# The same steps of a fused attention and MLP kernel in another written-out order

## The chip, the cores and the metric

One core of a Trainium2 chip. The metric is the device time of one execution in microseconds; a version's time is the median of several runs. TensorE does the matmuls, VectorE (DVE) and ScalarE (ACT) the elementwise work, GpSimd (POOL) issues the loads that change the type on the way, and SyncE (SP) issues the stores and the transposing loads.

## The reference

```python
def _attn_ref(q, k, v, tau):                       # 4 x 6080 x 256 each
    qn = q / (np.linalg.norm(q, axis=1, keepdims=True) + 1e-06)
    kn = k / (np.linalg.norm(k, axis=1, keepdims=True) + 1e-06)
    s = kn.transpose(0, 2, 1) @ qn / tau           # 256 x 256 per batch
    s = s - s.max(-1, keepdims=True)
    a = np.exp(s)
    a /= a.sum(-1, keepdims=True) + 1e-09
    return (v @ a).astype(np.float32)

def _moe_ref(x, w_in, w_out):                      # 24320 tokens, 256 -> 2048 -> 256
    h = x @ w_in
    c = np.float32(np.sqrt(2.0 / np.pi))
    g = 0.5 * h * (1.0 + np.tanh(c * (h + 0.044715 * h * h * h)))
    return (g @ w_out).astype(np.float32)
```

The output of the first, as 24,320 rows of 256, is the input of the second.

## The kernel before

**Tiling.** Per batch, q and k are read in pieces of 512 rows, cast to bf16 while they are loaded (`load_one`, L243), and summed up on TensorE into a 256 x 256 product (`gram_row`, L290) and, over squares on ScalarE and VectorE (L253) and folds on VectorE (L272), into column norms. A short chain of small steps turns these into the 256 x 256 attention matrix, which is multiplied into the first MLP matrix (`aw_part`, `aw_copy`, L497 to L515). So the rest is an MLP over v: 25 blocks of at most 1,024 tokens, each in two halves `t` of 512 (480 and fewer at a batch's end).

**One block.** v is cast to bf16 into a DRAM buffer by GpSimd (`cast_v`, L306) and from there loaded with a transposition by SP (`load_vt`, L319). The first matrix product is done either piece by piece (`j` steps, L553, with their GELU `J` on ScalarE, L564) or in sets that spend seven matmuls in place of eight (`small`, L613, with the steps of `set_step`, L636, on ScalarE and VectorE; they need sums of weights, L587, and differences of v, `vs0` to `vs2`, L602). The second product again spends seven products in place of eight (`product`, L727, with the differences of `sums_g`, L708). Its results are turned on VectorE in blocks of 32 x 32 (`turn`, L764, L768) into an output buffer `ot`, and SP stores a half with four issues of 128 KB (`store`, L771, L782). There are three `ot` buffers (L70), so the turn that begins a fourth half waits until the store of an earlier one has landed.

**What sets the order.** Everything after the first batch's attention runs in the order of one text, `ORDER` (L962), of 4,017 steps, worked off by the loop at L951. Each engine executes its own instructions in that order, and waits at each for what it needs; so do the queues of GpSimd and SP. A step is written `block:step` or `bN:step` for work on batch N: `14:j30` is the matmul of block 14, piece 3, half 0; `15:s3cq` is the ScalarE copy in set 3 of block 15 that opens a bank; `13:c11` is the turn of one quarter of block 13's output into half 0, `c12` and `c22` go to half 1; `12:O1` is the store of block 12, half 1; `lv` is a cast of v, `lt` a transposing load, `lq` and `lk` casts of q and k. These loads are not issued at once when their buffer is free: each also waits for the matmul that stands before it in the order (`GATE`, set at L296, L537, L560, L628, L739 and used in `after`, L92):

```python
    def after(inst, gate):
        if gate is not None:
            tc.add_manual_dep(inst.ins, gate.ins.name, mybir.DependencyInfo(
                mybir.DependencyClass.Sync, mybir.DependencyReason.DATA), reason="pace")
```

So the place of a load in the text sets the time at which it goes out.

Of the kernel before, what the change touches and what calls it, by code (L numbers as in the profile page):

```python
# [967 lines left out]
0:J50 :pA12 0:J51 :pF0 0:j71 0:j41 0:j60 0:j61 0:s6ap 0:J61 1:j00 0:J60 0:s7m1 b0:w13 0:s6m7 :pF1
0:s6ax 0:J71 1:j30 0:M1A 1:J00 1:J30 0:s7m5 1:j50 0:s6m3 0:J41 0:jb0 0:s7y5 b1:lk1 0:T3a 0:M1B
0:s7cq 0:s6G1 8:lv0 0:s7m6 0:s6m4 0:s7m2 b1:r0.0 0:Jb0 b0:w01 b1:lq2 1:J50 b1:r0.1 0:T1a 0:s7ap  # L970
1:j21 0:s7m3 0:s7G0 1:j10 0:T2a :pS1 b1:lk3 0:s6Gx b1:r0.2 0:s6Gr 3:lv0 1:j51 0:s7m7 0:s7ax 1:j41
0:s7G1 1:j31 :pS4 1:J21 1:J10 b1:r0.3 1:j40 1:J41 0:x1 0:s7Gx b1:lk2 0:s7m4 :pS2 1:vs0 1:j11 b1:dk0
b1:r1.0 b1:r1.1 b1:lq3 1:J11 1:J40 0:s7Gr 0:M2A 1:s3m1 0:T3b 1:vs1 b1:r1.2 1:s3cq 0:M6A 0:T1b 2:lv0
1:s3m2 b1:zq1 b1:lk4 b1:r1.3 1:J51 1:j01 b0:w03 0:M2B 1:J01 1:J31 1:s4m1 0:T2b 1:s3m6 4:lv0 1:s3m5
:pNA 0:M5A 0:M5B 1:s3G0 b1:lq5 0:c11 1:s4m5 1:s3y5 b1:zq0 b1:r2.0 b1:r2.1 0:M6B 1:s3ap b1:r2.2
b1:lq4 1:s4cq 1:vs2 1:s4m2 0:y5 b1:r2.3 1:s3m3 1:s3m7 0:T4b b1:r3.0 b1:zk1 1:s4y5 1:s3G1 1:s4m6
1:s4G0 0:ap b1:r3.1 1:s3ax b1:lk5 0:M3A 1:s4ap b1:f0.1 1:s3m4 1:s3Gx 1:s5m1 0:T4a 1:s4m7 0:M3B
1:s5cq 1:s3Gr b1:zq2 1:s5m2 1:s4ax 0:M7A 1:s5m5 1:s4m3 1:s5G0 1:s4Gx 0:c12 b1:r3.2 1:s5m6 1:s5y5
b1:f1.1 b1:dk4 1:s4m4 1:j20 1:s6m1 0:M7B 1:s4G1 1:s4Gr 1:J20 2:lt1 1:s5ap 1:s6cq 1:s5m3 1:s5m7
1:s7m1 b1:r3.3 b1:f1.2 1:s6m5 b1:r4.0 2:lt0 1:s6m2 0:ax 1:s5G1 1:s6m6 b1:r4.1 1:s5ax 1:s6y5 1:s5m4  # L980
1:s6G0 1:s5Gx b1:dk2 0:M4A 1:s6ap 1:s6m7 1:s7m5 b1:f2.1 1:s7cq b1:r4.2 1:s6ax 1:s5Gr b1:zq3 1:T3a
1:s6m3 0:M4B 1:s7y5 0:c21 b1:r4.3 1:s7m6 1:s6m4 1:s6Gx 1:M1A 1:s7m2 1:s6G1 1:s7ap 2:j11 1:s7m7
1:s7m3 b1:lq8 1:M1B 1:T1a 1:s7ax 2:j21 1:s6Gr b1:lq6 1:s7G0 b1:zq4 1:T2a 1:s7m4 1:s7G1 b1:lk6 2:vs0
1:x1 2:j00 b1:lk7 1:s7Gr 0:c22 b1:r5.0 2:j10 1:s7Gx 2:s2m1 2:J21 3:lv1 2:vs1 1:T3b b1:lq7 2:J00
1:M2A 2:J10 2:J11 1:M2B 2:j01 1:c11 2:s2cq 2:j30 2:j20 2:s2m5 2:s2m2 2:J01 2:s2m6 2:J30 2:J20 2:s3m1
1:T1b 2:s2G0 1:M6A 1:M5A 0:O1 1:T2b 2:s2y5 2:s3cq 2:s2ap 2:s3m5 b1:zk3 2:s3y5 2:s3m6 2:s2m7 2:s2m3
2:s2G1 2:s3m2 b1:f1.3 2:vs2 1:M5B 2:s2ax b1:f3.1 2:s3G0 2:s4m1 2:s2m4 1:y5 2:s4cq 1:M6B 2:s3ap
2:s2Gr 2:s3m7 2:s4m2 b1:zk5 b1:f3.2 1:ap b1:r5.1 2:s4m6 3:lt1 b1:r5.2 b1:r5.3 2:s4m5 1:T4b b1:f3.3
1:M7A 2:s4G0 2:s2Gx 2:s4y5 1:M7B 2:s3ax b1:zq5 2:s3Gx 2:s5m5 b1:r6.0 2:s4ap 2:s3m3 2:s3G1 2:s3m4
b1:f3.4 2:s3Gr b1:f5.1 2:s4m3 2:s4G1 1:M3A 3:lt0 2:s5m1 2:s4m7 2:s5cq 1:M3B 2:s5m2 1:T4a b1:r6.1  # L990
2:s5m6 2:s5y5 b1:zq6 1:ax 2:s5G0 1:M4A 2:s4ax 3:j11 0:O0 b1:f4.1 2:s5ap 2:s4Gx 3:j31 1:c12 3:J11
# [6 lines left out]
3:s3m1 3:J21 3:j00 3:vs1 b1:zq7 3:J20 3:s2cq 3:J00 b1:r8.0 b1:lq10 3:s2y5 2:M5A 3:s2m6 2:T2b b1:r8.1
3:s2m2 3:s3cq 2:M5B 3:s2ap b1:zq8 3:s2m7 b1:f5.4 3:s3m2 3:s2G0 3:s3G0 3:vs2 3:s2m3 2:y5 b1:r8.2
3:s2G1 b1:dk8 2:M6B 3:s3m5 3:s3y5 3:j10 3:s3m6 3:s2ax 3:s2m4 1:O1 2:ap b1:f7.1 3:s3ap 3:s2Gx 2:T4a  # L1000
2:M3A 4:lt0 3:J10 3:s4m1 3:s2Gr 2:T4b 2:M3B b1:zq9 3:s3m7 3:s3ax 3:s4m5 3:s4cq 3:s4y5 b1:zk9 2:c12
2:M7A 3:s4m2 3:s3m3 b1:r8.3 3:s4m6 2:M7B 3:s4ap 3:s4G0 3:s3G1 3:s5m5 4:lt1 3:s3m4 2:ax 3:s4m3 3:s3Gx
# [6 lines left out]
3:s7Gx b1:r11.3 3:s7G1 4:j20 b1:f9.2 2:O0 3:M1A 4:s3m1 4:vs0 6:lv1 4:J00 4:J20 4:J21 3:T3b 3:M1B
b1:gc 4:s2m5 4:vs1 4:s2cq 3:s7Gr 3:x1 4:j10 4:s2y5 b2:lk2 b1:f9.3 b1:zq10 3:T1b 3:T2a 4:s2m6 4:s2m2  # L1010
3:M5A 4:s2ap 3:M5B 3:M2A 4:s2m3 b1:zq11 3:T2b 4:s2m7 3:M2B 4:J10 4:s3m5 1:O0 4:s2G1 4:s2G0 4:vs2
4:s2ax 3:M6A 4:s3cq 4:s3m6 4:s3y5 3:y5 4:s2m4 4:s2Gr 4:s3m2 4:s2Gx 5:lt1 3:M6B 4:s4m1 b1:zk11 3:c11
3:T4b 4:j11 4:s3ap 4:s3G0 4:s3m7 3:ap 4:s4m5 4:s3m3 4:J11 b1:f9.4 4:s4cq 3:M3A 3:M7A 4:s3ax 4:s4y5
4:s3G1 4:s5m1 4:s4m2 b2:lk0 b1:f11.1 6:lv0 4:s4m6 4:s4G0 b2:lq0 4:s3m4 3:T4a 3:M3B 4:s4ap 4:s5m5
# [18 lines left out]
5:s7Gr 5:s7Gx 5:M1B 6:J50 5:T3b 6:j51 6:j21 6:s3G0 7:lt1 5:M5A 5:x1 5:T1b 6:J51 4:O0 3:O0 6:J21
6:s3m5 6:s3y5 6:s3m6 6:s4cq 5:T2a 7:lt0 5:M2A 6:s4m5 5:M2B 5:T2b 6:s3ap b2:zq0 5:c11 5:M5B b2:zq1
6:vs2 5:M6A 6:s3m7 6:s3ax 6:s4y5 6:s4m6 6:s3m3 6:s4ap b2:zk1 5:M6B 6:s5m5 6:s3m4 5:y5 5:ap 6:s4m2
6:s3G1 6:s4m7 6:s3Gx 6:s4m3 5:T4a 6:s4G1 6:s4ax 6:s4G0 7:j01 5:M3A 6:s3Gr 6:s5m1 6:s5cq 5:M3B 6:s5y5
5:M7A 5:T4b b2:f1.1 6:s5m6 6:s5m2 6:s4Gx 6:s4m4 6:s6m1 7:J01 6:s5G0 6:j30 5:M7B 5:c12 b2:lq3 6:s4Gr
6:s5ap 6:s6cq 6:s5m3 6:j10 b2:dk0 6:J30 6:s6m6 6:s7m1 6:s5m7 5:ax 6:s5G1 6:s6m5 6:j31 b2:zq2 6:s5ax
# [255 lines left out]
```

## Time and profile before

| | before |
|---|---|
| median of 3 runs | 690.88 us (690.78 to 691.38) |
| profiled execution | 690.03 us, span 688.3 us |
| mean granted clock of TensorE | 0.995 |
| busy TensorE / VectorE / ScalarE / GpSimd | 663.0 / 625.6 / 635.1 / 88.2 us |
| matmul records | 3410 |
| stores of 128 KB on SP, to landing | 160, median 3.0 us |
| transposing loads on SP, to landing | 47, median 3.1 us |
| casts of 256 KB (v, k, q) on GpSimd, to landing | 37, 33, 33, median 5.1, 5.9, 5.4 us |

Busy time is the time that an engine's instructions cover; in `x4` lines of a timeline several instructions are merged. The first 37 us belong to the first batch's attention and are outside `ORDER`. GpSimd's and SP's issues are not counted as busy. The time of a transfer runs from its issue to the moment its last part has landed.

### The profile page before, as it was taken

Reading aid. Unit: us, or ns where it says so; the run is one execution under the profiler, and the core shown is the slowest. Engines: PE = TensorE matmul, PEld = TensorE weight load, DVE = VectorE, ACT = ScalarE, POOL = GpSimd, SP = SyncE. Lnnn points to the kernel's source line nnn. Section 1 sums busy time; section 2 is a strip of 40 time slices with the busy share of each in tenths; the row PEclk is TensorE's granted clock in tenths of the full one; section 3 lists DMA queues with packets and bytes.
Section 4 is the critical chain, followed back from the end, with each engine's and each line's share of the span. In section 5 each row is a group of like instructions: output and inputs, shape, how many; then the busy total and the mean of one; then the engine's idle time right before and its main releaser. Section 6 shows DMA issues by size and latency. Waiting matters only on the chain.

```text
span 688.3 us, 10199 instructions
## 1 busy us (share of the span) xinstructions
PE 663.0 (96%) x3410; PEld 334.4 (49%) x3471; DVE 625.6 (91%) x922; ACT 635.1 (92%) x1224; POOL 88.2 (13%) x163
## 2 busy tenths in 40 slices
PE   3999999999999999999999997999999999999996
...
PEclk9999999999999999999999998999999999999999
...
GB/s 241 208 264 158 106 137 159 118 129 108 78 138 104 108 163 135 170 60 147 94 65 80 173 111 118 142 90 63 75 107 62 62 57 130 54 54 84 74 49 103
DMA packets 165093, 78.80 MB, mean 114 GB/s; under 512 B 148992, under 2 KB 153472, under 8 KB 164320
## 3 DMA queue, kind: packets, MB, share of 16 engines
...
## 4 chain that ended last, share of the span: by engine, by line
PE 86%; DMA 6%; ACT 5%; DVE 1%; issue 1%; SPq 0%; POOL 0%; DVEq 0%; POOLq 0%
PE u L739 22%; PE rb L628 16%; PE j L560 13%; PE p L739 12%; PE qb L628 8%; PE c L739 5%; PE G L296 4%; PE qa L628 4%; DMA qk<-in_k_dram 2%; DMA out_dram<-ot 2%; PE awp L501 2%; DMA qk<-in_q_dram 1%; ACT g L572 1%; ACT g L662 1%; ACT qa L643 1%
## 5 line engine op out<-in xcount | busy, mean ns | idle before, releaser
L739 PEld LDWEIGHTS <-wcomb 128*128 128x128 bf16 x1400 | 136.9, 98 | 146.9 <-issue 2.7
L739 PE MATMUL u<-t,wcomb 128*128 128x512 bf16 (+3 forms) x583 | 143.3, 368 | 0.8
L560 PE MATMUL j<-vT,aw 128*128 128x512 bf16 (+2 forms) x447 | 124.0, 375 | 0.8 <-DVE aw L392 0.5
L572 ACT ACTIVATE g<-j 128x512 bf16<-128x512 f32 (+1 forms) x204 | 122.0, 661 | 2.5 <-PE j L560 2.5
L648 DVE TENSOR_TENSOR qb<-rb,yw 128x512 f32<-128x512 f32 (+2 forms) x137 | 92.6, 679 | 10.4 <-PE rb L628 5.8
L651 DVE TENSOR_TENSOR xw<-rb,yw 128x512 f32<-128x512 f32 (+2 forms) x137 | 91.4, 669 | 7.5 <-PE rb L628 5.5
L628 PE MATMUL rb<-tv,sw 128*128 128x512 bf16 (+2 forms) x269 | 97.6, 375 | 0.6 <-DVE qb L648 0.2
L662 ACT ACTIVATE g<-xw 128x512 bf16<-128x512 f32 (+2 forms) x137 | 92.8, 680 | 5.6 <-DVE xw L651 5.6
L739 PE MATMUL p<-g,wcomb 128*128 128x512 bf16 (+3 forms) x394 | 96.6, 370 | 0.6
L646 ACT ACTIVATE yw<-qb 128x512 f32<-128x512 f32 (+2 forms) x137 | 87.6, 645 | 2.4 <-PE qb L628 2.2
L643 ACT ACTIVATE qa<-rb 128x512 f32<-128x512 f32 (+2 forms) x137 | 87.8, 643 | 2.2 <-PE rb L628 1.6
L653 ACT ACTIVATE g<-qa 128x512 bf16<-128x512 f32 (+2 forms) x137 | 87.6, 648 | 1.6 <-PE qa L628 1.3
L656 ACT ACTIVATE g<-qb 128x512 bf16<-128x512 f32 (+2 forms) x137 | 87.6, 644 | 1.5 <-PE qb L628 1.2
L659 ACT ACTIVATE g<-rb 128x512 bf16<-128x512 f32 (+2 forms) x137 | 87.2, 647 | 0.8 <-PE rb L628 0.6
L628 PEld LDWEIGHTS <-sw 128*128 128x128 bf16 x548 | 53.8, 98 | 56.4 <-issue 1.7
L560 PEld LDWEIGHTS <-aw 128*128 128x128 bf16 x456 | 44.3, 98 | 45.5 <-issue 1.1
L628 PEld LDWEIGHTS <-aw 128*128 128x128 bf16 x411 | 40.3, 98 | 42.7 <-issue 0.6
L720 DVE TENSOR_TENSOR t<-g,g 128x2048 bf16<-128x2048 bf16 (+3 forms) x50 | 58.0, 1160 | 1.0 <-ACT g L662 0.9
L722 DVE TENSOR_TENSOR t<-t,g 128x2048 bf16<-128x2048 bf16 (+3 forms) x50 | 57.4, 1157 | 1.2 <-PE u L739 1.1
L712 DVE TENSOR_TENSOR g<-g 128x2048 bf16<-128x2048 bf16 (+3 forms) x50 | 58.0, 1159 | 0.3
L718 DVE TENSOR_TENSOR t<-g,g 128x2048 bf16<-128x2048 bf16 (+3 forms) x50 | 57.9, 1161 | 0.2
L628 PE MATMUL rb<-tv,aw 128*128 128x512 bf16 (+2 forms) x137 | 51.1, 376 | 4.3 <-DVE xw L651 4.1
...
## 6 DMA issues: line engine op xcount, KB each, us to landing
out_dram<-ot SPq DMA_DIRECT2D x160, 128.0 KB, 3.0
...
wst<-in_moe_w_out_dram POOLq DMA_DIRECT2D x2, 1024.0 KB, 11.4
...
```

The costliest lines, as they stand in the source:

```text
L560: GATE[0] = nc.tensor.matmul(hp[:, :n].rearrange("p (t x) -> p t x", t=2) if t == 2 else hp[:, :n], lhsT=AW[b][:, cc, fc * 128 : fc * 128 ...
L572: nc.scalar.activation(g[:, t, fc % 8, :hc], hp[:, :hc], AF.Gelu_apprx_tanh)
L628: GATE[0] = nc.tensor.matmul(acc[:, :hc], lhsT=lhs, rhs=rhs, start=i in (1, 5), stop=True, skip_group_check=True)
L643: nc.scalar.activation(Q0[m, p][:, :hc], RB[m, p][:, :hc], AF.Copy)
L646: nc.scalar.activation(YW[m, p][:, :hc], Q1[m, p][:, :hc], AF.Copy)
L648: nc.vector.tensor_add(Q1[m, p][:, :hc], RB[m, p][:, :hc], YW[m, p][:, :hc])
L651: nc.vector.tensor_add(XW[m, p][:, :hc], RB[m, p][:, :hc], YW.pop((m, p))[:, :hc])
L653: nc.scalar.activation(g[:, 0, e, :hc], Q0.pop((m, p))[:, :hc], AF.Gelu_apprx_tanh)
L656: nc.scalar.activation(g[:, 1, e, :hc], Q1.pop((m, p))[:, :hc], AF.Gelu_apprx_tanh)
L659: nc.scalar.activation(g[:, 0, e + 1, :hc], RB.pop((m, p))[:, :hc], AF.Gelu_apprx_tanh)
L662: nc.scalar.activation(g[:, 1, e + 1, :hc], XW.pop((m, p))[:, :hc], AF.Gelu_apprx_tanh)
L739: GATE[0] = nc.tensor.matmul(ACCS[m, acc][:, :hc], lhsT=wcomb[:, w, fc, :], rhs=x[:, fc, :], start=first and k_ == 0, stop=k_ == 3, skip_g ...
```

## The change

Only the text of `ORDER` differs. It holds the same 4,017 steps, each as often as before, at other places from its first line on; the functions, the buffers and the sizes are the same. Each engine's instructions are the same in number and kind and stand in another order. Two stretches of it, around the stores of blocks 12 and 13, half 1:

```diff
...
-13:s4ax 13:s4G0 b3:r4.0 b3:lq8 12:ax 13:s5G1 13:s4G1 13:s4Gx b3:r4.1 13:s4m4 b3:dk4 12:c22 13:s6m1
-13:s5ax 13:s6cq b3:r4.2 12:M4A b3:lq6 12:M4B 13:s6y5 b3:lk8 13:s6m6 13:s4Gr 13:s5Gx 13:s6m2 13:s7m5
-b3:r4.3 13:s7m1 12:O1 b3:r5.0 13:s6G0 b3:lk7 17:lv1 13:s5m4 b3:f5.1 12:c21 13:s6ap 14:j30 13:s7cq
-13:T3a 13:s6m7 b3:r5.1 b3:lq7 13:s7m2 13:s7m6 13:s7y5 13:s6ax 13:s7ap 13:s5Gr 13:s6m3 13:s7G0 14:J30
-14:j31 13:s6m4 14:j20 13:T1a 13:s6G1 13:s7m7 b3:r5.2 14:s2m1 18:lv0 13:s7m3 13:M1A 13:s6Gx 13:s6Gr
-14:J31 13:s7ax 14:s2cq b3:f3.4 13:s7m4 13:s7G1 b3:r5.3 13:M1B b3:f4.1 14:J20 14:j21 13:s7Gr b3:lk9
-b3:lq9 13:x1 14:vs0 13:s7Gx 14:s2m2 14:j01 14:vs1 14:s2m5 14:s2m6 13:M2A 13:M2B 13:T2a b3:f5.2
...
+b3:zq4 12:ax 13:s4Gx 13:s6m5 b3:f5.1 12:c22 13:s6m2 12:O1 b3:lk6 13:s5ax 13:s4m4 b3:r4.3 13:s6m6
+13:s6y5 13:s4Gr b3:lq8 12:M4A 13:s6ap b3:lk8 b3:f3.4 13:s7m1 13:s6G0 12:M4B 13:s7cq 13:s5m4 17:lv1
+12:c21 b3:f4.1 b3:r5.0 13:s7m5 b3:lq7 13:s6m7 13:s6m3 b3:r5.1 13:s7m6 14:j31 13:s5Gx 13:s7m2 13:s5Gr
+b3:r5.2 13:s6G1 13:s7y5 14:j30 13:s6ax 13:s7G0 13:s6Gx 13:s6m4 b3:lk7 13:M1A 13:s7ap 14:J31 13:s7m7
+13:s7m3 14:j20 14:s2m1 13:T3a 13:s6Gr 18:lv0 b3:r5.3 14:J30 13:s7ax 13:s7m4 13:s7G1 14:J20 13:s7Gr
+13:T1a 13:M1B 14:j21 14:s2cq 14:vs0 b3:r6.0 14:s2m5 13:x1 14:j01 14:s2m2 14:vs1 13:T2a 14:s2m6
...
+14:s6m1 14:J10 b3:r7.2 14:s4Gx 13:T4a 14:s5m7 14:s6cq 13:c12 14:s5m3 14:s5ax 14:s6m5 14:s5G1 13:O1
+17:lv0 b3:dk8 b3:lk11 13:M4A 14:s7m1 14:s6m6 14:s6y5 14:s7cq b3:lq9 14:s5m4 14:s6m2 14:s6ap 13:M4B
+14:s5Gr 14:s6G0 b3:f7.1 14:s7m6 14:s5Gx 14:s7m5 14:s6m7 14:s6m3 13:c21 b3:lk9 14:s7y5 14:s6ax
+14:s6G1 15:j21 15:j00 15:J21 b3:r7.3 15:j30 14:s7ap 14:s6m4 14:s7m3 14:T3a 14:j00 b3:f7.2 15:J00
+14:s7m7 15:j01 18:lv1 b3:lq11 14:s6Gx 14:s7ax 14:s6Gr 14:J00 15:j20 b3:r8.0 14:s7G1 b3:r8.1 14:s7m4
+15:s2m1 15:J01 14:M1A 14:s7m2 15:J30 14:s7Gx 15:J20 b3:lq10 14:T1a 15:vs0 15:s2cq b3:r8.2 14:s7Gr
+15:vs1 15:s2m5 14:M1B 14:s7G0 b3:f7.3 b3:lk10 15:j31 14:x1 15:s2m6 15:s2m2 15:j11 15:s2y5 15:s2G0
+15:J31 b3:r8.3 b3:zk9 14:M2A 15:J11 14:T2a 15:s3m5 14:T3b 14:M2B 15:s3y5 b3:r9.0 15:s3m1 15:s2ap
...
```

More of the change, by code (lines that the diff above doesn't have):

```diff
@@ L968 @@
[L968 to L991, printed above, removed]
@@ L998 @@
[L998 to L1002, printed above, removed]
@@ L1009 @@
[L1009 to L1014, printed above, removed]
@@ new lines @@
+b1:f1.3 0:M4A 1:T3a 1:s5Gr 1:s6ax 1:s7ap 1:s6m4 1:s6Gx 1:s7m2 1:s7m7 b1:zq3 1:T1a 1:s7m3 b1:lk6
+0:M4B 1:s7ax b1:f3.1 1:s6Gr 1:s7G0 b1:r4.3 1:s7G1 b1:lq6 2:j21 0:c21 2:j30 b1:lq7 b1:r5.0 1:x1 3:lv1
+1:s7Gx 1:s7m4 2:J30 2:j20 2:j01 3:lt1 1:s7Gr 1:M2A b1:f3.2 2:j10 2:J21 2:J20 2:J01 2:s2m1 1:M2B
+2:vs0 1:T3b 2:s2cq 2:J10 1:T1b 2:vs1 2:s2m5 2:j00 2:s2m6 2:s2y5 1:c11 2:vs2 2:s2m2 b1:dk4 2:s2ap
+2:j11 2:s2G0 2:J11 1:M5A 2:s3m1 1:M5B 1:T2a 1:T2b 2:s2m7 2:s2ax 2:s3m5 2:s2m3 b1:zq4 0:O0 1:M6A
+b1:r5.1 1:M6B 2:J00 2:s2m4 0:c22 1:y5 2:s3cq 2:s2G1 b1:r5.2 b1:zq5 2:s3m6 2:s4m1 2:s3m2 1:ap 1:M7A
@@ new lines @@
+2:s7m1 3:J21 b1:r6.3 3:J10 2:s7cq 2:s6m3 2:T3a 2:s6m7 2:s7m5 b1:r7.0 2:s6G1 2:s6G0 b1:f5.2 b1:r7.1
+2:s6ax b1:r7.2 2:s7m2 3:j11 2:s7m6 2:s6m4 2:s7y5 2:M1A 2:s5Gr 3:s2m1 3:J11 b1:f6.1 3:j01 2:s6Gx
+2:s7ap 2:s6Gr 5:lv0 2:s7m7 b1:f5.3 2:s7m3 2:M1B 2:s7G0 3:j00 2:T1a 2:s7G1 b1:r7.3 2:s7ax 2:s7m4
+3:J01 3:j20 2:x1 2:T2a 2:s7Gx 3:vs0 b1:zq7 b1:lq10 2:T3b 2:s7Gr 2:M2A 3:J00 3:J20 3:s2cq 2:M6A
+b1:lq11 b1:f5.4 b1:lk9 b1:zk7 3:vs1 3:j30 2:M2B 3:s2m5 3:J30 3:s2m2 2:M5A 3:s2y5 2:T1b 2:c11 b1:lk11
+2:M5B 2:T2b 3:s2G0 2:y5 3:s3m1 3:s2m6 b1:f7.1 3:s3cq 3:s2ap 3:vs2 2:M6B b1:zq9 3:s3m5 3:s3y5 2:ap
@@ new lines @@
+4:s2m2 4:s2y5 3:M5B 3:T2b b1:zq10 4:s3m1 4:J21 3:M6B 4:s3m5 4:s2G0 4:s2ap 4:s2m7 b2:lq2 3:y5 4:s3cq
+3:T4b 4:s3y5 4:vs2 3:M2B 4:s3m6 4:s2m3 4:s2ax 3:ap 3:c11 4:s2m4 b1:zk11 4:s3ap 4:s2G1 4:s2Gr 4:s3m2
+4:s3G0 4:s2Gx b2:lk2 b1:f9.4 b1:f10.1 3:M7A 4:s4m5 4:j11 4:s4m1 4:s3m3 4:s3m7 b1:f11.1 4:J11 4:s4cq
+3:M3A 4:s3ax 4:s4m6 6:lv0 4:s3G1 4:s4y5 4:s4m2 b1:f11.2 8:lv1 4:s5m1 4:s4ap 4:s3m4 b1:f11.3 4:s4G0
+4:s5cq 4:s3Gr 3:M3B 3:T4a b1:f11.4 4:s4m3 4:s5m5 4:s3Gx 6:lv1 4:s5m2 5:j11 3:M7B 4:s5y5 5:J11 4:s4m7
@@ L1033 @@
[L1033 to L1038, printed above, removed]
@@ new lines @@
+6:s7Gr 7:s2m2 7:vs0 6:j00 7:j21 b2:r1.3 9:lv0 7:vs1 7:s2m5 7:s2G0 b2:r2.0 b2:r2.1 6:J00 6:s7Gx
+7:s3m1 7:s2y5 7:J21 6:T3a 6:T1a 7:J00 b2:r2.2 6:M1A b2:r2.3 7:s2m6 7:s3cq 6:M1B 7:s3m2 b2:r3.0
+b2:lq6 7:J10 6:x1 7:j31 7:s2ap 7:s2m3 7:s3G0 b2:lq5 7:J31 7:s2m7 7:s3m6 7:s2G1 7:s3m5 7:vs2 6:M2A
+b2:lk4 7:s5m1 6:T3b 7:s2ax 6:T2a 7:s3y5 7:s3ap 6:M2B 7:s2m4 6:M5A 6:T1b 7:s2Gx b2:lk6 b2:zk3 7:s2Gr
+b2:zq3 7:s3m7 6:c11 7:s3ax 7:s3m3 7:j30 6:M5B 7:s3m4 6:T2b 7:s5cq 7:J30 6:y5 6:M6A 6:T4a b2:f3.1
+7:s5m2 7:s3Gr 7:s4m1 7:s3G1 6:M6B b2:r3.1 7:s4cq 7:s5m6 7:s4m5 7:s4m6 6:ap 7:s4m2 7:s5G0 6:T4b
@@ new lines @@
+8:j30 7:s6Gr 7:s7m4 b2:r5.2 8:J20 8:j10 7:s7G0 7:T1a 7:M1A 7:s7G1 10:lv1 8:J30 b2:lq7 8:vs0 7:s7Gr
+8:s2m1 8:J10 7:s7Gx 8:j21 8:s2cq 7:M1B b2:f5.1 8:s2m5 7:T2a 8:j01 8:J21 7:x1 8:s2m2 8:vs1 b2:f4.1
+7:T3b 8:J01 7:T1b 8:s2m6 8:s2y5 8:s2G0 b2:r5.3 b2:r6.0 8:s2ap 8:vs2 8:s3m1 7:M2A 8:s3m5 8:s3cq
+b2:r6.1 b2:r6.2 7:T2b 7:M2B 8:s3m2 8:s2m3 8:s3y5 8:s2m7 8:s2ax b2:zq8 7:M6A 8:s3G0 8:s3m6 8:s2m4
+8:s2G1 7:c11 8:s3ap b2:dk6 8:s4m1 8:s4m5 9:lt1 7:M5A 8:s3m7 b2:r6.3 8:s2Gx 8:s2Gr 7:M5B 7:T4a 8:s4y5
+8:s4cq 8:s4m6 b2:zq6 8:s4m2 8:s3m3 7:M6B 8:s3ax 8:s3m4 7:y5 8:s4ap 8:s4G0 8:s3G1 10:lt0 8:s3Gx
@@ new lines @@
+8:s7ax 9:J11 7:c21 8:s7G0 8:M1A 9:j01 7:O0 9:s2m1 b2:lk11 8:s7m3 7:c22 11:lv1 b2:zq10 8:s7m4 8:s7Gx
+9:j21 b2:r8.1 9:s2cq 8:M1B b2:r8.2 b2:f7.3 8:s7Gr 9:vs0 b2:f7.4 9:J21 8:s7G1 b2:r8.3 9:J01 9:j10
+11:lv0 9:vs1 9:J10 b3:lq2 9:vs2 9:j00 9:s2m6 b2:lq11 12:lv1 b2:r9.0 8:T3b 9:s2m5 b2:r9.1 9:s2y5
+9:s2m2 8:T2a b2:r9.2 b2:r9.3 9:J00 9:s2ap 8:T1b 8:x1 b2:zk9 8:M5A 9:s3m1 8:M2A 9:s2m3 9:s2G0 9:s2m7
+9:s2G1 b2:dk10 9:s2ax b2:zq9 8:M2B 8:M5B 8:c11 9:s2m4 9:s3m5 8:T2b b2:f9.1 9:s3cq 9:j30 9:s3m2
+b2:f9.2 8:y5 9:s2Gr b3:lk1 9:s3y5 8:M6A 9:s3G0 9:s3m6 9:J30 9:s3ap 9:s4m1 9:s4cq 8:M6B 9:s2Gx 9:s4m5
@@ new lines @@
+9:s6m3 10:J00 9:s7m6 b2:ss 9:s6ax 10:s2m1 9:s5m4 9:s7G0 9:s7ap 9:s6G1 9:s6Gx 9:s6m4 9:s7m7 10:s2cq
+9:s7m3 9:T3a 9:s6Gr 9:M1A 10:s3m1 b2:sv 9:s7ax 9:s7G1 b2:pow 10:j01 10:s2m2 9:T1a 9:s5Gr 9:s7m4
+10:s3cq 10:J01 10:j30 9:M1B 10:j10 10:vs0 10:J30 9:M5A 9:s7Gx 9:s7Gr 10:vs1 b2:kf 10:vs2 10:s3m6
+10:J10 9:T3b 10:s2m6 9:T2a 9:T1b 9:x1 10:s3m2 13:lt1 10:s2m5 8:O1 9:M2A 9:M2B 10:s2G0 10:s3m5
+10:s2y5 10:s3G0 10:j31 10:s2ap b2:kr 9:c11 10:s3y5 9:M5B 10:s2m7 10:J31 10:s3ap 10:j11 10:s2ax
+10:s2m3 9:y5 10:s3m7 10:s3m3 11:lt1 10:s4m1 10:s2G1 9:M6A 10:s3G1 10:J11 9:T2b b2:krp 10:s4m5 b2:S0
@@ new lines @@
+10:s7m6 11:J01 10:s7y5 10:s6m4 b2:rc2 10:s7m2 10:s7G0 10:M1A 10:s7ap 10:s5Gr 10:s6Gx b2:eT 10:s6m3
+11:j10 10:s7m3 10:s7m7 11:J10 10:M1B b2:aw5 12:lt1 9:c21 10:s7ax 10:T3a 10:s7m4 b2:rsum 11:vs0
+10:s7G1 10:s6Gr 10:s6G1 10:x1 10:s7Gr b2:aw7 11:j30 b2:aw3 11:J30 10:M2A 10:s7Gx b2:rs b2:aw1 10:T1a
+9:c22 b2:ac5 b2:ac3 b2:ac1 10:T3b 11:s2m1 b2:aw2 b2:aw6 b2:ac2 13:lt0 11:vs1 b2:aw0 10:M5A 11:s2cq
+b2:ac6 10:M2B b2:ac0 10:T1b 11:s2m2 11:s2G0 9:O1 b2:aw4 10:M5B b2:ac4 11:s2m5 10:T2a 12:lt0 11:s3m1
+b2:ac7 11:j21 11:s2m6 11:s3m5 10:c11 11:s2y5 10:M6A 11:vs2 10:T2b 10:y5 11:s3cq 11:s2ap 11:s3y5
@@ new lines @@
+b3:r9.1 b3:f8.1 14:T1b 14:c11 14:M6A 15:s2m7 b3:zq9 15:s2m3 15:j10 15:s3cq b3:r9.2 b3:f7.4 b3:r9.3
+16:lt1 15:s3m6 15:s2ax 15:s3m2 15:s2G1 14:M5A 15:vs2 b3:zq11 15:s3ap 15:s3G0 12:O0 14:T2b b3:f9.1
+15:s2m4 14:M5B 15:s4m1 14:M6B 15:J10 14:T4b 15:s4m5 b3:r10.0 15:s2Gr 15:s2Gx 15:s3m3 14:y5 15:s3m7
+14:ap 15:s4cq b3:r10.1 15:s4m2 15:s3ax 15:s4y5 15:s3G1 15:s4m6 14:M3A 15:s4ap 15:s4G0 15:s3m4
+15:s5m1 b3:zq10 15:s4m7 b3:dk10 15:s3Gr 14:M3B 15:s5m5 14:T4a 15:s3Gx 15:s5cq 15:s4m3 14:M7A 15:s4ax
+15:s5m6 13:O0 15:s4m4 15:s5m2 14:c12 15:s5y5 b3:f9.2 15:s4G1 15:s5ap 15:s6m5 b3:f10.1 15:s6m1 14:M7B
@@ new lines @@
+15:s7Gx 16:J01 15:x1 16:s2y5 16:vs1 16:s2G0 15:T1a 16:s2m6 16:J20 16:j31 17:lt0 15:T3b b3:sv 16:s2ap
+16:vs2 16:J31 15:M2A 16:j11 16:s3m1 16:J11 15:T1b 16:s3m5 16:j30 16:s2m7 16:s2m3 15:M2B 16:s3cq
+16:s2G1 b3:pow 16:s2ax 16:s3y5 16:s3m6 15:M5A 16:J30 16:j00 b3:kf 16:s2m4 16:s3ap 14:O0 15:T2a
+16:s2Gx b3:kr 16:J00 16:s3m2 16:s2Gr 16:s3m3 16:s3m7 15:c11 16:s3ax 16:s3G1 15:M5B b3:krp 17:lt1
+16:s4m1 15:y5 16:s5m1 16:s3G0 15:T2b 16:s3m4 16:s3Gr 16:s5m5 b3:S0 b3:S1 16:s4cq 15:T4a b3:th1
+15:M6A 16:s5cq 15:M6B 16:s4m5 16:s4m2 15:ap 16:s4m6 16:s5y5 16:s5m6 b3:th0 16:s5ap 16:s4y5 16:s5m2
```

455 lines of the change are left out of this document (215 added, 240 removed).

## The prediction

> **What bounds the kernel now.** I read the slices of the page first, then the waits, then the timeline around the one slice that stands out. The row of TensorE and the row of its granted clock:
>
> ```profile
> PE   3999999999999999999999997999999999999996
> PEclk9999999999999999999999998999999999999999
> ```
>
> After the start every slice is full but one, near 420 us, where the clock is low too. The list of waits has only two causes that hold VectorE or TensorE for over a microsecond in the main part:
>
> ```profile
> DVE ot L768 <- DMA out_dram<-ot: 6.8, 2, 5.6
> ...
> PE rb L628 <- DVE xw L651: 4.1, 1, 4.1
> ```
>
> VectorE twice waited for a store to land, because a turn (L768) writes the output buffer `ot` that the store still reads; in one case TensorE then waited for VectorE. The timelines of TensorE and of VectorE there (start, us, engine, line):
>
> ```profile
> 418.72 1.03 PE L739 MATMUL p<-g,wcomb 128*128 128x512 bf16 x4
> 423.80 0.59 PE L628 MATMUL rb<-tv,aw 128*128 128x512 bf16 x1 [4.06 <-DVE xw L651]
> ...
> 427.46 1.65 PE L739 MATMUL p<-g,wcomb 128*128 128x512 bf16 x4
> 428.95 0.38 PE L628 MATMUL rb<-tv,sw 128*128 128x512 bf16 x1
> ```
>
> ```profile
> 416.48 0.41 DVE L611 TENSOR_TENSOR tv<-vT,tv 128x512 bf16<-128x512 bf16 x1
> 422.46 0.72 DVE L768 STREAM_TRANSPOSE ot<-c 128x512 f32<-128x512 f32 x1 [5.56 <-DMA out_dram<-ot]
> ```
>
> A 512-column matmul starts every 0.216 us at full clock, so TensorE should have gone on at 419.59 and did at 423.80: **4.21 us**. Windows of 1 us (busy, count, granted clock, DMA share, GB/s) show what follows:
>
> ```profile
> 421.00:422.00 1.00, 0.00 (x0) 0.94 0.26 46
> 422.00:423.00 1.00, 0.00 (x0) 0.50 0.01 2
> ...
> 428.00:429.00 1.00, 1.00 (x5) 0.64 0.90 170
> ```
>
> From about 421.9 to 428.7 the clock is halved. Between 423.80 and 428.95 stand nine 512-column and six 256-column matmuls, 2.59 us at full clock, that took 5.15: **2.56 us** more. The other store wait is smaller, near 259 (VectorE):
>
> ```profile
> 258.76 0.72 DVE L768 STREAM_TRANSPOSE ot<-c 128x512 f32<-128x512 f32 x1 [1.22 <-DMA out_dram<-ot]
> ```
>
> Two matmuls there start 0.69 and 0.38 us late: **1.07 us**, clock unchanged. Together 7.84 us. To see if anything else is lost I added up the matmuls of the order from its first (37.76 us) by width: 0.216 us per 512 columns, 0.2025 per 480, 0.109 per 256, 0.22 for each single fp32 column. The last should start 9.2 us earlier than it does; 7.84 are these two waits, the remaining 1.4 lie in some twenty gaps of 0.05 to 0.2 us. **TensorE is the bound, and store landings are what interrupts it.**
>
> **Why those stores were late.** A store is four issues, and the store that held VectorE for 5.6 us was issued from 405.18 to 406.72; the table of `out_dram` for that time:
>
> ```profile
> DMA to landing us min/median/max: 4.8/8.0/15.6
> ```
>
> The usual landing is 3.0 us (the same table over the run). GpSimd had issued ten cast loads between 402.93 and 414.77; the last landed at 422.5, the store's last issue at 422.3. The same holds elsewhere: eight casts from 242.7, the store's last issue lands at 258.6; nine from 377.3, 395.3 (harmless, its buffer is wanted 6 us later). So **a store inside a bunch of casts lands when the bunch is worked off, 1.94 to 2.0 us per cast of 256 KB**, counted from the bunch's first issue.
>
> **The change, part by part.** All 4,017 steps of the order stay, each once; instructions per engine, matmul widths and DMAs are equal. Only positions move, so the same 636 us of matmuls remain, and the sum is about waits alone. I placed every DMA of the changed order by the matmul or step that it waits for, at that matmul's counted time, plus the 0.4 us by which GpSimd's issues follow their gate in the trace of before; a store's first issue stands 0.7 us behind the counted place of its last turn, as the rows of SP mostly do there, and its four issues 0.55 us apart. Times of the changed order below are counted ones, with no stall.
>
> *Removed, the wait near 259.* The store of block 5, half 0, is issued at 239.3 to 241.0, before the casts from 243.2; its buffer is wanted at 256.5. Seven casts from 243.2 now meet the store of block 6, half 1; it lands by 257 and its buffer is wanted at 264.9. −1.07 us.
>
> *Removed in part, the wait near 417.* The store of block 12, half 1, is issued at 403.5 to 405.2 among seven casts (403.0, 403.6, 404.5, 405.8, 406.3, 408.6, 410.5), where it had ten. 403.0 + 7 × 1.94 to 2.0 = 416.6 to 417.0. Its buffer goes to the turn `13:c11`, counted at 417.3. The first matmul that needs that turn is counted at 417.74 and needs 0.9 us after the landing (0.12 to the turn's start, 0.72 turn); the next, at 418.18, needs 1.46 after (422.34 to 423.80 in before). No loss up to a landing at 416.7. A straight line through before's bunches with a fixed part (5.6 + 1.4 per cast) gives 418.4 and a loss of 1.7. I take 0.5, the end nearest to the rows of eight and nine casts. −6.77 + 0.5.
>
> *Added, a wait near 444.* A new bunch starts at 429.8: casts at 429.8, 430.3, 430.9, 431.4, 433.2, 436.2, 436.8, 437.3, 438.6, 439.9, two of them of 32 KB and two of 192 KB, 7.7 full ones. The store of block 13, half 1, falls right in, at 429.9 to 431.5. 429.8 + 7.7 × 1.94 to 2.0 = 444.7 to 445.2 (446.2 with the fixed part). Its buffer goes to the turn `14:c11` at 443.7. Behind it on VectorE wait `vs2`'s difference (needed by TensorE at 446.91) and on ScalarE the copy `15:s3cq` (counted 444.3, needed by TensorE at 445.83, 1.65 us after a landing). No loss up to 444.2; 0.5 to 2.0 beyond, more if VectorE, with 16.5 us of work given to it in the 15 us from 427.8, can't catch up. I take 1.5. Were the store to land in 3 us, nothing: bounds 0 and 4.2, what before paid at 420.
>
> *Everything else.* Transposing loads and cast loads have to arrive in time. In before the least margin between a landing and the first reader is 0.9 us (a k load at 56), without loss. Here the least is the transposing load of block 1: cast at 43.3, transposed from 51.1, landing 55 to 56.4 (before 56.4), reader at 56.6. The next are 1.7 (block 2) and 1.8 us (a q load at 49). Five stores have their buffer wanted 5.9 to 6.3 us after the last issue (near 455, 524, 622, 673 and 674) but no cast near, so at 3.0 us they land 2 us early. TensorE's waits on VectorE and ScalarE stand no closer behind what they wait for than before (the 5% quantile of matmul time between them: 0.42 and 0.86 us, before 0.22 and 0.85). Price: 0, bounds 0 and 3. The end (last matmul to end 5.3 us) has the same steps.
>
> Sum against the profiled execution: 690.03 − 7.84 + 0.5 + 1.5 = 684.2. The median of the runs shown is 0.85 above that execution, so **685.0 us**.
>
> **A rule weighed.** At 258 to 262 a wait of 1.07 us left the clock at 1.00; near 420 the clock fell 2.3 us after TensorE's work ran out. So a wait of 1.5 us should cost no clock, one over 2.3 may. [...]
>
> **Rivals.** (1) *Both remaining waits vanish*: casts that come later in a bunch don't hold a store already under way. For: the store at 277 landed in 7.5 us with ten casts about it. 690.88 − 7.84 = 683.0. (2) *The step order itself adds small waits*, VectorE near 430 to 450 above all; 1.5 to 4 us more: 686.5 to 689. (3) *The wait near 444 grows past 2.3 us and halves the clock*: 3 + 2.6 instead of 1.5: 689.1. (4) *Slower*: a store's last issue takes its own 15.0 to 15.6 us whenever seven or more casts are about (as with 9, 9.6 and 10 casts), not the bunch's time. Then 405.2 + 15.6 = 420.8 and 431.5 + 15.6 = 447.1, losses 4.1 and 2.9, each with 2.56 of halved clock: 12.2 against 7.84, **695.2**; it turns slower once both waits pass 2.3 us and halve the clock (landings after 419.0 and 446.5). Against: with eight casts it was 9.5. (5) *The change does not keep casts apart*: true around 404 and 430, and priced above.
>
> **Chances.** Forecast (684 to 686.5) 0.42; (1) 0.25; (2) 0.15; (3) 0.09; (4) and the like 0.09. A measurement of this kernel tells 0.2% (1.4 us) from no change: faster 0.83, same 0.08, slower 0.09. Range 682.6 to 689.0: it leaves out (4), and half of (3).
>
> **What would show it.** No VectorE wait on a store near 259; at 417 one under 2 us; a store of block 13 that lands near 445 and a TensorE gap of 1 to 2 us there, clock 1.00. Wrong if TensorE loses time where no store is in flight, or if these two stores take 15 us.

## The result and the profile after

The changed kernel takes **683.58 us** (median of 4 runs, 683.11 to 683.72); the kernel before, run beside it, 690.83 us (690.70 to 691.38). The ratio is 0.989 (95% interval 0.9875 to 0.991): faster, by 7.2 us or 1.1 per cent. The profiled execution of the changed kernel took 683.62 us, its span is 681.8 us.

The two rows of its page, TensorE's busy share and its granted clock, in 40 slices:

```profile
PE   3999999999999999999999999999999999999997
PEclk9999999999999999999999999999999999999999
```

The slice near 420 us that stood at 7, with 8 below it for the clock, is full. In the list of waits the cause that had 6.8 us in two waits is down to one:

```profile
DVE ot L768 <- DMA out_dram<-ot: 1.9, 1, 1.9
```

It is the wait near 417 that the prediction reduced and did not remove. The timelines of the changed kernel there, VectorE's line first and then TensorE's (start, us, engine, line, idle time ahead and what ended it):

```profile
418.91 0.72 DVE L768 STREAM_TRANSPOSE ot<-c 128x512 f32<-128x512 f32 x1 [1.89 <-DMA out_dram<-ot]
```

```profile
418.49 0.38 PE L628 MATMUL rb<-vT,aw 128*128 128x512 bf16 x1
419.68 0.38 PE L628 MATMUL qb<-tv,sw 128*128 128x512 bf16 x1 [0.81 <-DVE ot L768]
...
421.99 1.02 PE L739 MATMUL p<-g,wcomb 128*128 128x512 bf16 x4 [0.49 <-DVE g L712]
```

The turn starts 0.12 us behind the landing of the last part of the store of block 12, half 1 (418.79). TensorE should have gone on 0.216 us after 418.49 and did at 419.68; with the gaps that follow until 421.99 it loses 0.98 + 0.15 + 0.65 = **1.78 us**. No VectorE wait on a store stands near 259 or near 444.

Counted as in the prediction (each matmul's real start against a gapless row of the same widths), TensorE loses 3.30 us from the first matmul of the order to the last, where it lost 9.21. The end behind the last matmul takes 5.03 us (5.39 before), and the first matmul starts 0.14 us earlier: 5.91 + 0.36 + 0.14 = 6.41 us, which is the difference of the two profiled executions, 690.03 - 683.62.

The store that was to bring the new wait, block 13, half 1, goes out from 432.31 to 433.77, with the casts that were named about it. The tables of `out_dram` for the four issues from 404.5 on and the four from 432 on:

```profile
L782 SPq DMA_DIRECT2D out_dram<-ot x4: 316/552/633, 404.6 to 406.2; - x4
...
DMA to landing us min/median/max: 3.9/11.5/12.8
```

```profile
L782 SPq DMA_DIRECT2D out_dram<-ot x4: 316/499/722, 432.3 to 433.8; - x4
...
DMA to landing us min/median/max: 2.3/6.8/8.8
```

The first lands at 418.8, as late as the seven casts about it (the last of them at 418.1). The second lands at 442.4, though the last cast of its bunch lands at 447.8. Its buffer was wanted at 446.1. So the forecast's rule, that a store lands when the bunch is worked off, holds for the first of these two stores and fails for the second.

### The profile page after: what moved, and what is told of

Read it like the earlier page. It is cut to its first block, busy times and chain, and to the rows that moved or that the text cites. A ratio compares the mean times of both kernels' runs of the same rounds, so it can differ in the third digit from the quotient of the medians.

```text
span 681.8 us, 10259 instructions
## 1 busy us (share of the span) xinstructions
PE 663.4 (97%) x3471; PEld 333.5 (49%) x3471; DVE 626.1 (92%) x922; ACT 635.2 (93%) x1224; POOL 87.8 (13%) x163
## 4 chain that ended last, share of the span: by engine, by line
PE 85%; DMA 6%; ACT 4%; DVE 3%; issue 1%; SPq 0%; POOL 0%; DVEq 0%; ACTq 0%; POOLq 0%
PE u L739 22%; PE rb L628 15%; PE j L560 13%; PE p L739 11%; PE qb L628 8%; PE c L739 5%; PE G L296 4%; PE qa L628 4%; DMA qk<-in_k_dram 3%; PE awp L501 2%; DMA out_dram<-ot 2%; DMA qk<-in_q_dram 1%; ACT sq L266 1%; ACT qa L643 1%; ACT g L572 1%
## 5 line engine op out<-in xcount | busy, mean ns | idle before, releaser
L739 PE MATMUL u<-t,wcomb 128*128 128x512 bf16 (+3 forms) x600 | 145.4, 368 | 0.0
L572 ACT ACTIVATE g<-j 128x512 bf16<-128x512 f32 (+1 forms) x204 | 127.0, 663 | 2.2 <-PE j L560 2.2
L560 PE MATMUL j<-vT,aw 128*128 128x512 bf16 (+2 forms) x456 | 126.6, 376 | 0.2 <-DVE aw L392 0.2
L309 POOL DMA_DIRECT2D vb<-in_v_dram x47 | 23.6, 503 | 222.1 <-PE rb L628 123.9
```

What stands on the lines that cost most here:

```text
L560: GATE[0] = nc.tensor.matmul(hp[:, :n].rearrange("p (t x) -> p t x", t=2) if t == 2 else hp[:, :n], lhsT=AW[b][:, cc, fc * 128 : fc * 128 ...
L572: nc.scalar.activation(g[:, t, fc % 8, :hc], hp[:, :hc], AF.Gelu_apprx_tanh)
L739: GATE[0] = nc.tensor.matmul(ACCS[m, acc][:, :hc], lhsT=wcomb[:, w, fc, :], rhs=x[:, fc, :], start=first and k_ == 0, stop=k_ == 3, skip_g ...
```

## The experiments

All runs, medians, each with its ratio to the kernel before on the same chip (691.06, 691.26 and 690.84 us beside the later runs). In the names `ot4` is a fourth output buffer, `thin` and `bunch` are casts moved away from a store and towards it, `512` are casts in smaller packets, `pool` is GpSimd issuing stores:

| run | us | ratio (95% interval) | lost by TensorE, us | end, us |
|---|---|---|---|---|
| before | 690.83 | | 9.21 | 5.39 |
| changed | 683.58 | 0.989 (0.9875 to 0.991) | 3.30 | 5.03 |
| changed, once more | 683.22 | 0.989 (0.987 to 0.990) | 3.01 | 5.00 |
| before_ot4 | 683.89 | 0.9895 (0.988 to 0.991) | 1.34 | 7.03 |
| after_ot4 | 683.09 | 0.988 (0.987 to 0.990) | 0.94 | 6.68 |
| before_thin | 685.61 | 0.992 (0.991 to 0.9935) | 4.51 | 5.35 |
| after_bunch | 687.29 | 0.9945 (0.993 to 0.996) | 6.91 | 5.04 |
| after_thin | 681.60 | 0.986 (0.985 to 0.988) | 0.83 | 5.01 |
| after_bunch2 | 685.17 | 0.992 (0.9895 to 0.9935) | 4.19 | 5.04 |
| before_512 | 684.86 | 0.991 (0.989 to 0.993) | 3.43 | 5.37 |
| ot4_pool | 683.98 | 0.990 (0.988 to 0.991) | 1.19 | 7.45 |

"Lost" is counted in the run's profiled execution as above; "end" is from the start of the last matmul to the end of the span.

**Are the store waits the whole difference?** A fourth buffer takes the waits away and leaves each order as it is.

```diff
-    yout = ctx.enter_context(tc.tile_pool(name="yout", bufs=3))
+    yout = ctx.enter_context(tc.tile_pool(name="yout", bufs=4))
...
-        c = cp.tile([128, HALF], FP32, tag=f"c{ci}", name=f"c{m}_{ci}{tj}")
+        c = cp.tile([128, HALF], FP32, tag="c1", name=f"c{m}_{ci}{tj}")
```

> The kernel before with a fourth output buffer, and nothing else moved (the room comes from one addend buffer that only the last block uses). Theory (the two waits for landing stores are the whole difference): the wait near 420, its halved clock and the wait near 259 go, though all casts stay bunched and the store of block 12, half 1, still lands about 15 us after its issue: 690.8 - 7.84 = 683.0 us (682.6 to 683.6), no VectorE wait on a store, clock 1.00. Rival (the gain comes from other moved steps): the order of before keeps losing time elsewhere, over 685.5 us.

> The changed kernel with the same fourth buffer. Theory: only its one wait of 1.78 us near 418 goes, 683.6 - 1.8 = 681.8 us (681.4 to 682.4), so the two orders with four buffers lie about 1 us apart, by small gaps. Rival (the changed order is better in its compute steps too): the orders differ by over 2.5 us with four buffers. Other rival (the wait at 418 only covers for something that is late next): within 0.5 us of 683.6.

Measured: 683.89 and 683.09 us. In the order of before the store of block 12 still lands 16.3 us after its last issue; nothing waits for it, the mean clock is 0.998 (before 0.995), and TensorE loses 1.34 us in place of 9.21. That is 7.87 us less, against the 7.84 that the prediction read from the two waits. The order of compute steps is therefore worth little: with four buffers the two orders lose 1.34 and 0.94 us. Both runs are about 1 us slower than expected and outside their ranges, by a thing no theory had: the end grew by 1.65 us in both (see the last experiment). So after_ot4 comes within 0.5 us of the changed kernel, the time of its second rival, but not for that rival's reason, as its loss did fall, from 3.30 to 0.94 us.

**Is it the casts about the store?** One order gets three casts fewer there, the other two more.

```diff
-14:s2m1 18:lv0 13:s7m3 ... 13:s7Gr b3:lk9 b3:lq9 13:x1
+13:M6B b3:lk9 b3:lq9 14:s4m6 ... b3:r6.3 18:lv0 b3:r7.0
```

> The order of before with three loads moved and nothing else: the casts of k and q chunk 9 and of block 18, half 0, which went out at 411.4 to 414.8 behind the store of block 12, half 1, now stand some 10 us later in the order, behind the turn that wants the buffer. Seven casts are left around the store. Theory: the store lands at 417.5 to 419 in place of 422.3, TensorE loses 0 to 0.5 us there and its clock stays whole: 690.8 - 6.8 + 0.3 = 684.3 us (684.0 to 685.5); the wait near 259 stays. Rival (a cast that is issued over 5 us after the store no longer holds it): landing and time as in before, 690 to 691. Rival (the other moved steps carry the gain): over 688.

```diff
-14:s7cq b3:lq9 14:s5m4 ... 13:c21 b3:lk9 14:s7y5
+14:j21 b3:lq9 b3:lk9 14:s2cq
```

> The changed order with two loads moved back into the bunch and nothing else: the casts of k and q chunk 9 stand 20 us earlier, where they stood in before, so that nine casts lie around the store of block 12, half 1. Theory: it lands near 422 in place of 418.8, TensorE loses 4.5 to 5.5 us there in place of 1.78 and its clock is halved for 2.5 us more: 683.6 + 5.8 = 689.4 us (687.5 to 690.5). Rival (a cast that is issued over 5 us after the store no longer holds it): 683.6, landing at 418.8.

Measured: 685.61 and 687.29 us, both in the direction of the theory and outside the two rivals, and both by less than expected, just outside the stated ranges. With three loads moved, before loses 4.51 us in place of 9.21. The store lands at 418.87, inside the forecast, but TensorE still loses 2.36 us there, as its first matmul behind the turn comes 1.47 us after the landing and a second gap of 0.71 follows; 0 to 0.5 had been expected. With two casts added, the changed order has its store landing at 421.31. The timelines of after_bunch, VectorE and then TensorE:

```profile
421.44 0.72 DVE L768 STREAM_TRANSPOSE ot<-c 128x512 f32<-128x512 f32 x1 [4.67 <-DMA out_dram<-ot]
```

```profile
418.23 0.38 PE L628 MATMUL rb<-vT,aw 128*128 128x512 bf16 x1
422.21 0.38 PE L628 MATMUL qb<-tv,sw 128*128 128x512 bf16 x1 [3.59 <-DVE ot L768]
```

A gap of 3.76 us, and behind it the clock is at 0.50 for 3.4 us (below). So two casts that were issued 7 us behind the store's last part (412.9 and 413.4) held it 2.5 us longer. The landing of the store of block 12, half 1, from the bunch's first cast on, in all runs but before_512: five casts 12.0 us (after_thin), seven 14.9 to 15.7 (the changed kernel twice, after_ot4, after_bunch2, ot4_pool) and 16.4 (before_thin), nine 17.7 (after_bunch), ten 19.4 and 20.0 (before, before_ot4).

**Can the last wait be taken away?**

```diff
-13:s5m4 17:lv1 12:c21 ... 13:s6Gr 18:lv0 b3:r5.3
+13:M7A 18:lv0 14:s5cq ... 14:j10 17:lv1 14:s5m6
```

> The changed order with two loads moved and nothing else: the casts of block 17, half 1, and of block 18, half 0, which went out among the seven around the store of block 12, half 1, now stand 14 to 20 us later, in a stretch without casts; they are first read 30 us after that. Five casts are left around the store. Theory: it lands by 416 to 416.7, the last wait on a store goes, 683.6 - 1.8 = 681.8 us (681.2 to 682.5). Rival (the matmuls at 417.7 wait for VectorE's work, not only for the landing): 682.8 to 683.6. Rival (the moved casts hold the next stores instead): a new wait near 427 to 430, over 683.6.

Measured: **681.60 us** (681.21 to 681.77), where the changed kernel on the same chip took 683.22. The table of `out_dram` for the four issues of block 12, half 1:

```profile
DMA to landing us min/median/max: 3.7/8.8/10.1
```

It lands at 415.4, no wait on a store is left, and TensorE loses 0.83 us over the whole order. This is the fastest version of the study.

**What holds a store inside a bunch?** Two theories were left. A: the store's last part lands when the bunch is worked off. B: the store's packets and the casts' packets take turns, about one for one. In the trace of before a store is 2,048 packets of 256 B, a cast of q or k 128 packets of 2,048 B that take 172 ns each where a store's take about 20 (medians over the run 173 and 18, the store's mean 22). If B holds, then while casts keep the 16 engines full, the store gets some 80 turns in a microsecond (an estimate: 16 turns of each in 172 + 20 ns), and how late it lands depends on how many of its packets are still to go. To tell them apart the casts were cut into four times as many packets, in the order of before:

```diff
-        after(nc.gpsimd.dma_start(out=t[:, 0:n, :], in_=source(which, b)[:, r0 : r0 + n, :]), gate)
+        after(nc.gpsimd.dma_start(
+            out=t[:, 0:n, :],
+            in_=(q, k)[which][b, r0 * 128 : (r0 + n) * 128, :].rearrange("(r p) c -> p r c", p=128)), gate)
```

> The order of before, unchanged, with the q and k loads of batches 1 to 3 read in another row order (partition p of a piece takes rows p, 128 + p, ... in place of neighbouring rows; the sums over rows are the same), so that a cast of 256 KB moves in 512 packets of 512 B in place of 128 of 2,048 B. Theory B (the store's packets and the casts' packets take turns, about one for one, so that a store of 2,048 packets gets little while 128 large packets per cast flow): the store of block 12, half 1, gets about four times as many turns beside q and k casts and lands near 411 to 414 in place of 422, though all ten casts stay around it; both waits go, 683 to 684 us. Theory A (the store's last part lands when the bunch is worked off): it lands with the last cast or behind it, 421 to 425, and the time is 690 or more. If small packets make the casts themselves much slower, both say more than 691, and the trace tells them apart.

Measured: 684.86 us. The table of the store of block 12, half 1, in before_512 (before: at most 15.6 us):

```profile
DMA to landing us min/median/max: 5.2/5.9/8.0
```

It lands at 415.6, 8 us ahead of the bunch's last cast (423.6): A falls. B holds in kind; 411 to 414 had been expected, and 683 to 684 us. The lists of DMA queues for a stretch with packets of casts of q and k and of stores show how many of each went (packets, MB, share; q0 are the casts, q1 the stores; in the second stretch a transposing load is issued too, whose packets also count in q1). First before, 254 to 256 us, then before_512, 255 to 258 us:

```profile
q0 software_dynamic: 190, 0.35, 93.0%
q1 hardware_dynamic: 232, 0.06, 19.8%
```

```profile
q0 software_dynamic: 743, 0.37, 89.8%
q1 hardware_dynamic: 729, 0.18, 46.0%
```

In both the stores' queue moves about one packet for one of the casts (1.2 and 0.98), at either size: 116 a microsecond beside packets of 2,048 B, 243 beside packets of 512 B. The casts pay for it, with 0.12 MB a microsecond in place of 0.175. So in these two stretches it is the packets that come out about equal, and not the bytes, which agrees with B; in which order the packets of the two queues ran the lists don't show. The casts' share is 93.0% and 89.8% there. From 409 to 412 us in before it is 79.1%, and the stores' queue moves 728 packets beside 217 of the casts, 3.4 for one. That the store's packets also fill the time that the casts leave free is my reading of these counts, and no run shows it.

The time of before_512 did not fall to 683 because the wait near 259 grew from 1.22 to 2.16 us: that store landed at 259.47, with the bunch's last cast (259.71), as theory A would have it. Three casts of v stand in that bunch, whose packets were not cut, and the k and q casts became slower (median landing 6.7 and 5.7 us, before 5.9 and 5.4). That these two made the wait longer is likely, but no run shows it.

The same lists for the changed kernel at the store of block 13, 434 to 436 and 436 to 438 us, suggest why that one landed early:

```profile
q0 software_dynamic: 17, 0.23, 96.0%
q1 hardware_dynamic: 70, 0.01, 5.0%
```

```profile
q0 software_dynamic: 172, 0.20, 59.3%
q1 hardware_dynamic: 717, 0.18, 41.8%
```

A cast of v comes as 16 packets, here of 15 KB (15,360 B); 15 of them start from 434 to 436 and take 2.05 us each in the mean, and the stores' queue moves 70 packets in all. In the next two microseconds the casts' share is 59.3%, GpSimd issues nothing between 435.85 and 438.86, and the stores' queue moves 717 packets. If that gap is what saved it, filling the gap must bring the wait:

```diff
-15:j01 18:lv1 b3:lq11 14:s6Gx ... 15:J20 b3:lq10 14:T1a ... b3:f7.3 b3:lk10 15:j31
+13:M4B 18:lv1 b3:lq11 14:s5Gr ... b3:r7.3 b3:lq10 15:j30 b3:lk10 14:s7ap
```

> The changed order with four loads moved and nothing else: the casts of block 18, half 1, of q chunk 11 and of q and k chunk 10, which went out 6 to 10 us after the store of block 13, half 1, now stand 0 to 3 us behind it, with the four that stood there already. Theory B (turns of packets): the store no longer gets its 1,000 free packets between 436 and 439, lands near 447 (446 to 449) in place of 442.4, and the turn of block 14 at 446.1 waits: the wait near 444 to 447 that was forecast, 1 to 2.5 us, 685.0 us (684.2 to 686.5). Rival (this store lands early because its first part goes out ahead of the casts, wherever the later ones stand): landing by 443, time 683.6.

Measured: 685.17 us, 1.95 us over the changed kernel on the same chip. The store of block 13, half 1, in after_bunch2, and the turn that wants its buffer:

```profile
DMA to landing us min/median/max: 2.3/7.3/13.8
```

```profile
447.87 0.72 DVE L768 STREAM_TRANSPOSE ot<-c 128x512 f32<-128x512 f32 x1 [1.56 <-PE qb L628]
```

The last part lands at 447.69, and the turn, which ran at 446.13 in the changed kernel, starts 0.18 us behind it. The profile puts this wait down to a matmul whose result the turn doesn't read; but the trace's records show VectorE's sequencer from 444.00 to 447.73 waiting on two counters for this turn, and one of them (109) is the counter of the store's last issue. TensorE loses 0.87 us at 449.31. That is the wait that had been forecast, and it takes casts closer together than the changed order has them. It is not the whole 1.95 us: the two profiled executions differ by 1.30 us (684.78 and 683.48), of which TensorE's loss has 1.18 (4.19 in place of 3.01).

> The changed kernel as it is, once more, on the chip of the three others: 683.6 us (683.1 to 684.0). If it differs by over 0.7 us, differences between the earlier runs and these of under 1 us carry no weight.

Measured: 683.22 us (682.91 to 684.19), 0.36 below the first.

**Why does a fourth buffer lengthen the end?** With four buffers SP's last six issues come late, in one row. The timeline of SP in after_ot4:

```profile
676.11 2.82 SPq L782 DMA_DIRECT2D out_dram<-ot  x6
```

The trace's records of ScalarE and SP there (start, ns, the counter waited for and the one counted up):

```
Scalar DMA_DIRECT2D 674.32 357 782 $S[107]>= semaphore=108
Sync EVENT_SEMAPHORE 676.06 17 782 $S[108]>=
Sync DMA_DIRECT2D 676.11 315 782 $S[107]>= semaphore=108
```

SP waits on counter 108, which ScalarE's store of block 24 uses; that store lands at 676.04. The program hands out eight counters in turn to the transfers of both queues (108 to 111 and 115 to 118 in the records of before and of the changed kernel), and with four buffers the turn falls so. The changed kernel has such a pair too: SP's last two stores go out from 678.71 on, just behind the landing (678.65) of ScalarE's store on counter 116, where ScalarE issued its stores of the same half from 677.56 on. That this lengthens its end, by up to 1.1 us, is an estimate from these records that no run tests.

```diff
-                eng = (nc.sync, nc.scalar)[bi % 2]
+                eng = (nc.sync, nc.gpsimd)[bi % 2]
```

> The changed kernel with four output buffers once more, and the half of block 24's stores that ScalarE issued now issued by GpSimd; nothing else differs. With four buffers the time fell by only 0.5 us in place of 1.8, because the end behind the last matmul grew from 5.0 to 6.7 us: SP's first issue for block 23, half 0, stood until 676.11, 0.07 us behind the landing (676.04) of ScalarE's first store of block 24, and the program gives the two the same completion counter. Theory (SP waits there for the counter alone): GpSimd's stores count on other counters, SP issues its stores at 672 to 674 again, the end takes 5.0 to 5.5 us, 683.1 - 1.3 = 681.8 us (681.4 to 682.4). Rival (SP's issues are late for another reason, such as the order in which the four buffers are given out): end at 6.5 us or more, 683 or more.

Measured: 683.98 us, the rival's time, but not the rival's reason. SP's two stores of block 23, half 0, now go out at 670.66 and 671.02, its last at 676.01, and the last transfer lands at 678.82, where it was 680.26 in after_ot4 and 680.86 in the changed kernel (3.9, 5.7 and 4.0 us behind the start of the last matmul). So the theory of the counter stands. The end is long for a new reason, in the records of the trace:

```
GpSimd DRAIN 676.35 5220 1289
GpSimd DMA_DIRECT2D 676.73 604 782
```

GpSimd's closing drain ends at 681.57, 4.24 us behind the end of its last issue and 2.75 behind the last landing; the span ends 0.8 us behind it, at 682.4. In the changed kernel GpSimd's last issue is at 673.54, and its drain is done at 678.04, before SP is.

## Why the prediction was right, and where it was wrong

Right: the bound, the mechanism (landing stores interrupt TensorE, and casts make them land late) and the sign. TensorE's loss was to change by -7.84 + 0.5 + 1.5 = -5.84 us and did by -5.91, but that agreement is luck: **two terms are off by over a microsecond each, and cancel**. The time, 683.58 us, lies inside the range and outside the narrower forecast of 684 to 686.5, near the 683.0 of rival (1), of whose two waits one vanished.

- *The 7.84 us of the two waits.* Right: 7.87 with a fourth buffer.
- *The wait near 259 removed, -1.07.* Right: no such wait is left.
- *The wait near 417, taken as 0.5.* Mis-sized: 1.78. The step that failed is "7 x 1.94 to 2.0" for the time from the first cast to the landing: 13.6 to 14.0 us, measured 15.0. I chose the price per cast of the rows with eight and nine; the line with a fixed part, 5.6 + 1.4 per cast, which I gave as the other end with a loss of 1.7, gives 15.4. It fits the five, nine and ten casts of the other runs too (12.6, 18.2 and 19.6 against 12.0, 17.7 and 19.4 to 20.0), and falls 1.0 short of the seven in before_thin.
- *The new wait near 444, taken as 1.5.* It did not come. The step that failed is the rule that a store inside a bunch lands when the bunch is worked off. What the runs point to is the number of casts' packets that run before the store's 2,048 are through: in this bunch 717 of these went from 436 to 438, in a gap of 3 us between issues; with that gap filled (after_bunch2) the store landed 5.3 us later, as the last cast did. I counted 7.7 casts from 429.8 on without looking at how their issues were spread, though the list has the gap (433.2 to 436.2). Rival (1) was right in its reason, that casts later in a bunch don't hold a store already under way, for this store only: in after_bunch two casts that were issued 7 us behind the store of block 12 held it.
- *Everything else, 0.* Nearly right: the small gaps go from 1.4 to 1.5 us in all.
- *The end, the same.* It took 0.36 us less; the start of the order 0.14 less. Among SP's closing waits before has a pause of 0.34 us, up to 687.31, that the changed kernel doesn't have; its cause stays open.
- *0.85 for the median over the profiled execution.* It was a property of one execution of before, not of the kernels: for the changed kernel the median lies 0.04 below. This is the largest part of the 1.4 us by which 685.0 is too high (0.89 here, 0.50 by end and start, 0.07 by the waits).

The clock kept whole through the 1.78 us (1.00 in each microsecond from 417 to 422), as forecast. But "the clock fell 2.3 us after TensorE's work ran out" is no fixed delay. In after_bunch the work runs out at 418.45; windows of 1 us there (busy and count of TensorE's matmuls, its weight loads, VectorE, ScalarE and GpSimd, then granted clock, DMA share and GB/s):

```profile
422.00:423.00 1.00, 0.79 (x4) 0.29 (x3) 1.00 (x3) 0.24 (x1) 0.00 (x0) 1.00 1.27 283
423.00:424.00 1.00, 0.95 (x4) 0.43 (x4) 1.00 (x2) 1.00 (x3) 0.00 (x0) 0.82 0.39 75
...
427.00:428.00 1.00, 1.00 (x6) 0.51 (x5) 0.68 (x2) 0.55 (x2) 0.00 (x0) 0.97 0.00 0
```

It falls near 423.65, 5.2 us after the work ran out and when TensorE has been busy again for 1.4 us, and is back near 427.06. The stretch at 0.50 is 3.4 us long, where before's was 6.8 (421.9 to 428.7). The trace's records of the clock have these as 3.413 and 6.827 us, and the full stretches around them, 402.773 and 259.413 us in before, 406.186 and 256.000 in after_bunch, are whole multiples of 3.4133 us as well (118, 76, 119 and 75), as is the 662.186 us of the changed kernel (194). A clock that changes only at such steps would agree with both 2.3 and 5.2 us; that is my estimate from these stretches, and no run tests it. Nor do the traces show how little work makes the clock fall: in the 3.4 us ahead of the fall at 423.65 TensorE's matmuls took 1.4 us, in those ahead of 421.9 in before 1.1. In the 3.4 us before that in after_bunch, which ended at 420.24, they took 1.6 us, and the clock stayed at 1.00.
